# A written-out instruction order, planned anew: head of a hash-attention and feed-forward kernel

## Chip, cores and metric

The kernel runs on one core of one Trainium2 chip. The metric is the device time of one execution in microseconds (us). The kernel before takes 305.61 us (median of 7 runs, 303.85 to 307.07).

## What is computed

For 4 batches, 8 heads, 768 positions and a head width of 64, attention is masked by a hash: query and key may meet only where the signs of their six projections agree. The result is laid out as 4 x 768 rows of 512, and goes through a layer norm, a feed-forward of width 2048 with ReLU, and a residual sum.

```python
q_bits = einsum('bhsd,dk->bhsk', q, proj) > 0        # k_bits likewise
mask   = all six bits of the query equal those of the key
attn   = softmax(where(mask, q @ k.T / 8, -1e9)) @ v
x      = attn as (batch, 768, 512)
out    = x + relu(layernorm(x) * g @ w1) @ w2
```

## The kernel before, in words

**Units and steps.** The output rows are cut into 12 units of 256 rows, three per batch. A unit's attention is six steps: two groups (g) of four heads, and in each three key blocks (kp) of 256 keys. Step s belongs to unit s // 6, group (s % 6) // 3 and key block s % 3; steps 0 to 5 are unit 0, steps 6 to 11 unit 1.

**One step.** `S` (line 443) is 24 matmuls on TensorE: for two halves of the key block, one product of the sign vectors (6 rows, tile G) and two of the values (32 rows each, tiles kb and qb), for four heads. The four heads lie in partitions 0, 32, 64 and 96, so that four matmuls stand in different rows of the array. The sign product raises allowed scores above the others, and the mask thus needs no instruction of its own. `E` (line 449) is the exponential on ScalarE (ACT), two instructions of two heads each. `A` (line 458) is 16 matmuls that add E times V into the PSUM tile `acc`.

**Scores in PSUM.** The scores of a step take two pairs of banks, one for two heads. There are two such pairs, scA and scB. The banks of `acc` can serve as a third pair as long as no sums stand in them; `SC_PAIRS` says for which steps they do.

**Preparing batch 0.** Loads `lx` bring q and k of batch 0 in pieces into tiles X; the vector engine (DVE) transposes a piece of 256 positions in two instructions, `tn` (line 246); `ca` (lines 253 to 257) casts it to bf16, on ACT, POOL (GpSimd) or DVE; `ha` (line 315), four float32 matmuls with the spread projection `pfull`, gives the products whose signs `bi` (line 249, DVE) writes into G. There are 12 such pieces: 2 groups, q or k, 3 blocks. `pf` (line 280, DVE) fills `pfull` from the small load `lp`. `sv` and `sw` sum V over the keys, for a tiny term that keeps the normalisation finite. Later batches use whole loads `LX`, transposes `tu`, casts `CA`, one matmul group `hm` (line 408), `bt`, and 16 small copies `mo` (line 420) into G.

**After a unit's attention** come `na`, `nb`, `nc` (lines 469 to 480; normalising, statistics), `ce` (483, 484), a transpose of the normed rows (on TensorE for unit 0: `ft`, line 498, evicted by `fc`; by DMA later: `fl`, line 493), `F` (line 511; eight matmuls give 256 of the 2048 hidden columns, so eight F per unit), `R` (ReLU, on ACT or DVE), `D` (line 527; four matmuls of the second product), `Z` and the stores `O`. `rs` (489, 490, POOL) is the inverse deviation. `gB` (line 327, word `lg`) is the layer-norm gain, first used by `ce`.

**Weights.** POOL issues eight loads `lw1.p.n` and `lw2.p.n` (lines 330, 333), each 512 KB of bf16 made from float32 on the way. F number p needs chunk p // 2 of w1; D quarter n needs chunk n of w2.

**What sets the order.** The schedule is manual. `ORDER` is a list of words; a word is an operation, an engine (v DVE, a ACT, p POOL, s SP, t TensorE) and its numbers. Each engine runs its words in the order of the list; SP runs the loads, copies and stores that it issues in that order too, and one that waits holds all behind it. Waits between engines follow from the data.

The words of before that start the work:

```
mem.v on.p.1 on.p.0 lp.a pf.v lx.s.0.1.1.3 tn.v.0.1.2 ca.p.0.1.2 tn.v.0.1.1 lx.s.0.0.0.1 tn.v.0.0.0 ca.a.0.0.0
ca.a.0.1.1 lx.s.1.0.0.1 warm.t ha.t.0.1.2 bi.v.0.1.2 tn.v.1.0.0 ca.p.1.0.0 ha.t.0.0.0 bi.v.0.0.0 lx.s.0.1.0.1
```

and how a word is run:

```python
with tc.manual_schedule():
    for word in ORDER.split():
        name, eng, *args = word.split(".")
        OPS[name](ENGINES[eng], *map(int, args))
```

`warm` is 46 small matmuls at the start whose result nobody reads.

Of the kernel before, what the change touches and what calls it, by code (L numbers as in the profile page):

```python
# [17 lines left out]
mem.v on.p.1 on.p.0 lp.a pf.v lx.s.0.1.1.3 tn.v.0.1.2 ca.p.0.1.2 tn.v.0.1.1 lx.s.0.0.0.1 tn.v.0.0.0 ca.a.0.0.0  # L18
ca.a.0.1.1 lx.s.1.0.0.1 warm.t ha.t.0.1.2 bi.v.0.1.2 tn.v.1.0.0 ca.p.1.0.0 ha.t.0.0.0 bi.v.0.0.0 lx.s.0.1.0.1
tn.v.0.1.0 ca.a.0.1.0 ha.t.1.0.0 bi.v.1.0.0 pmem.p p32.p S.t.2.2 E.a.2.1 E.a.2.0 lv.s.0.0.4 cv.p.0.0.2 ha.t.0.1.1  # L20
bi.v.0.1.1 ha.t.0.1.0 lx.s.1.1.0.3 tn.v.1.1.2 ca.p.1.1.2 S.t.1.2 E.a.1.1 E.a.1.0 lx.s.1.0.1.3 ha.t.1.1.2 bi.v.0.1.0
S.t.0.2 E.a.0.0 E.a.0.1 lg.s tn.v.1.1.1 ha.t.1.1.1 ca.p.1.1.1 bi.v.1.1.2 S.t.5.2 E.a.5.1 tn.v.1.1.0 ca.p.1.1.0
ha.t.1.1.0 cv.p.0.0.0 A.t.1.2 A.t.0.2 bi.v.1.1.1 lw1.p.0 E.a.5.0 S.t.4.2 E.a.4.1 lw1.p.1 lx.s.0.0.1.3 tn.v.0.0.2
tn.v.0.0.1 ha.t.0.0.1 ca.v.0.0.1 lw2.p.1 E.a.4.0 bi.v.1.1.0 sv.t.0 LX.s.1.0.1 tu.v.1.0.1.3 tu.v.1.0.1.1 tu.v.1.0.1.2
lw1.p.3 tu.v.1.0.1.0 lw2.p.0 CA.p.1.0.1.1 tn.v.1.0.2 A.t.2.2 bi.v.0.0.1 S.t.6.2 E.a.6.0 E.a.6.1 ha.t.1.0.2 sw.v.0
na.v.0.0 nb.v.0.0 S.t.3.2 nc.v.0.0 E.a.3.1 bi.v.1.0.2 ha.t.0.0.2 lv.s.0.4.4 cv.p.0.4.0 cv.p.0.4.2 sv.t.4 LX.s.1.0.0
tu.v.1.0.0.0 tu.v.1.0.0.2 lv.s.1.4.1 S.t.8.2 E.a.3.0 A.t.3.2 E.a.8.0 A.t.5.2 E.a.8.1 A.t.4.2 ca.v.1.0.2 tn.v.1.0.1
ca.v.1.0.1 bi.v.0.0.2 ha.t.1.0.1 S.t.7.2 E.a.7.1 E.a.7.0 LX.s.1.1.1 lw1.p.2 sw.v.4 na.v.0.1 nb.v.0.1 A.t.8.2
nc.v.0.1 A.t.6.2 ce.v.0.0 bi.v.1.0.1 ft.t.0.0 fc.a.0.0 S.t.10.2 E.a.10.0 E.a.10.1 ce.v.0.1 ft.t.0.1 rs.p.0
tu.v.1.0.0.1 A.t.7.2 fc.v.0.1 F.t.0.0 R.a.0.0 CA.v.1.0.0.0 LX.s.1.1.0 S.t.11.2 E.a.11.1 E.a.11.0 lw2.p.2  # L30
tu.v.1.0.0.3 CA.a.1.0.0.1 hm.t.1.0 bt.v.1.0 mo.s.1.0.3.0 mo.s.1.0.0.0 mo.s.1.0.2.3 mo.s.1.0.0.3 mo.s.1.0.1.2
mo.s.1.0.0.1 mo.s.1.0.1.3 mo.s.1.0.3.3 mo.s.1.0.0.2 F.t.0.7 R.v.0.7 lw2.p.3 S.t.9.2 E.a.9.1 CA.p.1.0.1.0 F.t.0.6
F.t.0.3 na.v.1.0 nb.v.1.0 A.t.10.2 ca.v.0.0.2 E.a.9.0 S.t.14.2 E.a.14.1 tu.v.1.1.0.3 A.t.9.2 R.v.0.6 mo.s.1.0.2.2
E.a.14.0 nc.v.1.0 R.v.0.3 lv.s.1.0.0 A.t.11.2 na.v.1.1 F.t.0.4 R.a.0.4 LX.s.2.1.1 F.t.0.1 R.a.0.1 S.t.13.2 E.a.13.0
E.a.13.1 nb.v.1.1 A.t.14.2 nc.v.1.1 ce.v.1.0 ce.v.1.1 fl.s.1.1 fl.s.1.0 F.t.0.5 R.a.0.5 tu.v.1.1.0.0 lv.s.1.4.2
F.t.0.2 R.a.0.2 LX.s.2.0.0 lv.s.1.4.3 lv.s.1.0.3 tu.v.1.1.0.1 mo.s.1.0.1.1 mo.s.1.0.1.0 mo.s.1.0.2.1 tu.v.1.1.1.3
S.t.12.2 E.a.12.1 E.a.12.0 tu.v.1.1.1.0 tu.v.1.1.0.2 CA.a.1.1.0.1 mo.s.1.0.2.0 lv.s.1.0.1 mo.s.1.0.3.1 LX.s.2.0.1
D.t.0.0.0 D.t.0.0.1 D.t.0.0.2 D.t.0.0.3 S.t.16.2 E.a.16.0 E.a.16.1 mo.s.1.0.3.2 tu.v.1.1.1.1 F.t.1.7 R.v.1.7
A.t.13.2 A.t.12.2 na.v.2.0 F.t.1.2 R.a.1.2 S.t.17.2 E.a.17.1 E.a.17.0 tu.v.1.1.1.2 CA.p.1.1.1.1 hm.t.1.1 Z.v.0.0
D.t.0.1.0 bt.v.1.1 mo.s.1.1.3.2 mo.s.1.1.3.0 mo.s.1.1.2.1 mo.s.1.1.1.1 mo.s.1.1.0.1 mo.s.1.1.0.0 mo.s.1.1.1.2  # L40
mo.s.1.1.3.1 F.t.1.0 R.a.1.0 S.t.15.2 E.a.15.0 E.a.15.1 rs.p.1 nb.v.2.0 nc.v.2.0 A.t.16.2 A.t.17.2 mo.s.1.1.0.3
# [24 lines left out]
tu.v.3.0.1.1 mo.s.2.1.1.1 cv.p.2.0.0 S.t.33.2 E.a.33.0 E.a.33.1 A.t.31.2 sa.p.2.0.2 mo.s.2.1.0.3 tu.v.3.0.1.3
F.t.4.5 R.a.4.5 tu.v.3.0.1.0 tu.v.3.0.0.3 CA.a.3.0.0.1 D.t.3.0.2 D.t.3.0.3 Z.v.3.0 F.t.4.3 R.a.4.3 CA.p.3.0.1.0
rs.p.4 tu.v.3.0.0.0 S.t.35.2 E.a.35.1 E.a.35.0 mo.s.2.1.1.2 F.t.4.6 R.v.4.6 D.t.3.1.0 O.s.2.1 CA.a.3.0.0.0
sa.p.2.0.1 sb.p.2.0 lv.s.2.4.2 lv.s.2.4.3 su.p.2.0 lv.s.2.4.1 lv.s.2.4.0 F.t.4.0 R.a.4.0 S.t.37.2 E.a.37.0 E.a.37.1
na.v.5.0 nb.v.5.0 A.t.35.2 A.t.34.2 nc.v.5.0 O.s.2.3 mo.s.2.1.2.0 F.t.4.2 R.a.4.2 tu.v.3.0.1.2 CA.a.3.0.1.1 A.t.33.2  # L70
na.v.5.1 nb.v.5.1 nc.v.5.1 ce.v.5.1 fl.s.5.1 cv.p.3.4.2 ce.v.5.0 fl.s.5.0 S.t.36.2 E.a.36.1 E.a.36.0 F.t.4.1 R.a.4.1
cv.p.2.4.0 D.t.3.1.1 D.t.3.1.2 D.t.3.1.3 Z.v.3.1 O.s.3.2 O.s.3.1 sa.p.2.4.2 mo.s.2.1.2.3 A.t.36.2 F.t.4.7 R.a.4.7
S.t.38.2 E.a.38.1 F.t.4.4 R.v.4.4 D.t.4.0.0 D.t.4.0.1 E.a.38.0 S.t.42.2 F.t.5.4 R.v.5.4 D.t.4.0.2 D.t.4.0.3 Z.v.4.0
sa.p.2.4.1 F.t.5.3 R.v.5.3 mo.s.2.1.3.3 A.t.38.2 on.p.3 E.a.42.0 sa.p.2.4.0 E.a.42.1 S.t.39.2 E.a.39.1 E.a.39.0
sp.t.2.0 sc.v.2.0 D.t.4.1.0 O.s.3.3 A.t.37.2 na.v.6.0 nb.v.6.0 nc.v.6.0 F.t.5.6 R.a.5.6 S.t.41.2 E.a.41.0 E.a.41.1
D.t.4.1.1 D.t.4.1.2 D.t.4.1.3 Z.v.4.1 O.s.4.1 O.s.4.0 O.s.4.2 O.s.3.0 F.t.5.2 R.a.5.2 S.t.40.2 E.a.40.0 F.t.5.0
R.v.5.0 cv.p.2.4.2 A.t.41.2 lv.s.3.0.1 A.t.39.2 lv.s.3.0.2 F.t.5.1 sb.p.2.4 su.p.2.4 E.a.40.1 S.t.44.2 E.a.44.1
# [42 lines left out]
def kernel(  # L120
# [15 lines left out]
    nc = tc.nc  # L136
    P = 128
    B, H, S, D = q.shape
# [11 lines left out]
    A = 4 * (D + 1)  # L150
    W = S // 4

    SC_PAIRS = {2: ("scA", "scB"), 0: ("acc", "scA"), 1: ("scB", "acc"), 4: ("scA", "scB"), 3: ("acc", "scA"), 5: ("scB", "acc")}
# [15 lines left out]
    p32 = pool.tile([P, 2, 32], F32, name="p32")  # L169
# [421 lines left out]
```

The softmax here doesn't subtract the row's maximum and nothing guards it: scores larger than these inputs give would overflow.

## Time and profile before

| | |
|---|---|
| median of 7 runs | 305.61 us |
| the profiled execution, its own time | 304.04 us |
| its span, first to last instruction | 302.3 us |
| TensorE matmul busy | 292.3 us, 97% |
| ScalarE busy | 194.5 us, 64% |
| VectorE busy | 170.0 us, 56% |
| GpSimd busy | 72.3 us, 24% |
| granted TensorE clock, mean | 1.000 |

PE is TensorE's matmul side, PEld its weight loads, DVE VectorE, ACT ScalarE, POOL GpSimd, SP the engine that issues most DMAs. A row of the timeline gives start and length in us, engine, line, operation, output and inputs, the count, and in brackets the idle time before it and who ended it. Matmuls overlap, so a row's length exceeds the distance to the next row, and a PE that is "busy" is not always at its peak; distances from start to start are the safer measure. "q" after an engine's name is its queue: SPq rows are issues of DMAs.

### The profile page before, as it was taken

The numbers are of one execution on the slowest core, as the hardware profiler recorded it, in microseconds if no ns is written. First come the engines' busy times: TensorE is split into PE (matmuls) and PEld (weight loads), VectorE is DVE, ScalarE is ACT, GpSimd is POOL, SyncE is SP. The second block draws the span as 40 slices with busy tenths as digits, with TensorE's granted clock in tenths as the row PEclk, the third lists the DMA queues.
The fourth block names the chain that finished last, engine by engine and source line by source line (L and its number), as shares of the span: only waits on it lengthen the run. The fifth ranks groups of instructions, "written<-read, shape, count | busy, mean of one in ns | idle before, by whom it ended". The sixth has DMA issues, their size and how long they took to land.

```text
span 302.3 us, 9838 instructions
## 1 busy us (share of the span) xinstructions
PE 292.3 (97%) x4319; PEld 205.0 (68%) x4360; DVE 170.0 (56%) x348; ACT 194.5 (64%) x215; POOL 72.3 (24%) x112
## 2 busy tenths in 40 slices
PE   8999899999999999999999999999999999999994
PEld 7667676675766677676667677776657667685673
DVE  4678878377258527766345767555217446266012
ACT  2977789657667787786567676557667767561320
POOL 2791500202661005241600520911000101001000
PEclk9999999999999999999999999999999999999999
DMA  7999996936164275516306100310402103403122
GB/s 196 376 342 308 208 205 158 263 112 170 47 167 109 55 219 156 103 74 146 87 2 176 38 8 8 75 42 19 89 2 72 37 2 19 105 4 74 30 72 69
DMA packets 30426, 33.58 MB, mean 111 GB/s; under 512 B 15536, under 2 KB 27056, under 8 KB 30384
## 3 DMA queue, kind: packets, MB, share of 16 engines
q1 hardware_dynamic: 25792, 28.50, 35.3%
q0 software_dynamic: 4224, 4.19, 8.5%
q8 instruction: 34, 0.56, 0.8%
q10 hardware_dynamic: 368, 0.26, 0.3%
q14 instruction: 8, 0.07, 0.1%
HBM read 27.53 MB, written 6.29 MB: 112 GB/s over the span
## 4 chain that ended last, share of the span: by engine, by line
PE 88%; DMA 4%; DVE 2%; SPq 2%; ACT 1%; issue 1%; DVEq 0%; ACTq 0%
PE f L511 29%; PE sc L443 17%; PE acc L458 11%; DMA X<-in_q_dram 4%; PE hp L408 3%; ACT E L449 1%; SPq L294 1%; PE f_100None L527 1%; PE f_101None L527 1%; PE f L527 1%; PE f_00None L527 1%; PE f_11None L527 1%; PE f_80None L527 1%; PE f_51None L527 1%; PE f_01None L527 1%
## 5 line engine op out<-in xcount | busy, mean ns | idle before, releaser
L449 ACT ACTIVATE E<-sc,bias_sb 128x1024 bf16<-128x1024 f32 x144 | 153.0, 1110 | 49.2 <-PE sc L443 48.1
L511 PE MATMUL f<-xnT,w_sb 128*128 128x256 bf16 x768 | 99.3, 273 | 0.3
L511 PEld LDWEIGHTS <-w_sb 128*128 128x128 bf16 x768 | 70.9, 98 | 22.9 <-issue 7.7
L519 ACT ACTIVATE hb<-f 128x512 bf16<-128x512 f32 x57 | 33.9, 596 | 44.3 <-PE f L511 44.2
L527 PEld LDWEIGHTS <-hb 128*128 128x128 bf16 x400 | 37.7, 98 | 34.4 <-issue 2.7
L521 DVE TENSOR_SCALAR hb<-f 128x512 bf16<-128x512 f32 x39 | 26.9, 689 | 46.1 <-PE f L511 45.8
L443 PE MATMUL sc<-qb,kb 32*128 32x256 bf16 x1152 | 52.2, 267 | 0.0
L458 PEld LDWEIGHTS <-E 128*128 128x128 bf16 x1152 | 40.0, 98 | 6.4 <-issue 3.8
L458 PE MATMUL acc<-vaug,E 128*128 128x65 bf16 x1152 | 43.4, 194 | 0.1
L443 PE MATMUL sc<-G 6*128 6x256 bf16 x576 | 41.7, 273 | 0.8 <-DVE G L249 0.3
L489 POOL TENSOR_SCALAR rs<-mv 128x2 f32<-128x2 f32 x12 | 7.1, 594 | 104.8 <-DVE mv L483 104.5
L443 PEld LDWEIGHTS <-kb 32*128 32x128 bf16 x1152 | 30.2, 93 | 1.6
L443 PEld LDWEIGHTS <-G 6*128 6x128 bf16 x576 | 15.2, 91 | 18.8 <-issue 15.6
L246 DVE STREAM_TRANSPOSE T<-X 128x384 f32<-128x384 f32 x48 | 24.8, 553 | 3.3 <-DMA X<-in_k_dram 1.1
L469 DVE SCALAR_TENSOR_TENSOR acc<-vsB,acc 128x520 f32<-128x520 f32 x24 | 16.8, 701 | 15.1 <-PE acc L458 14.8
L356 POOL TENSOR_TENSOR t<-vn 128x256 f32<-128x256 f32 x18 | 13.3, 749 | 34.8 <-DMA vn<-in_v_dram 34.6
L346 POOL CAST vaug<-vn 128x768 bf16<-128x768 f32 x16 | 13.1, 829 | 26.5 <-DMA vn<-in_v_dram 21.5
L484 DVE SCALAR_TENSOR_TENSOR xc<-x,mv,gB 128x512 bf16<-128x512 f32 x24 | 18.9, 788 | 0.9
L480 DVE BATCH_NORM_STATS2 st<-x 128x6 f32<-128x256 f32 x48 | 18.0, 417 | 0.7
L476 DVE TENSOR_TENSOR x<-acc,rc 128x512 f32<-128x512 f32 x24 | 16.6, 691 | 0.8
L257 POOL CAST kb<-T 128x768 bf16<-128x768 f32 x10 | 8.4, 841 | 28.6 <-DVE T L246 28.6
L315 PE MATMUL hf<-tp,pfull 128*128 128x256 f32 x48 | 13.2, 401 | 0.4 <-DVE tp L246 0.4
(98 smaller groups left out, 224.1 us busy)
## 6 DMA issues: line engine op xcount, KB each, us to landing
out_dram<-x SPq DMA_DIRECT2D x44, 128.0 KB
X<-in_k_dram SPq DMA_DIRECT2D x7, 768.0 KB
X<-in_q_dram SPq DMA_DIRECT2D x6, 768.0 KB
vn<-in_v_dram SPq DMA_DIRECT2D x24, 192.0 KB
w_sb<-in_moe_w_ch_dram POOLq DMA_DIRECT2D x8, 512.0 KB, 16.6
vn<-in_v_dram SPq DMA_DIRECT2D x2, 768.0 KB
G<-B SPq DMA_DIRECT2D x96, 4.5 KB
X<-in_q_dram SPq DMA_DIRECT2D x2, 512.0 KB
```

Source lines behind the costliest of these rows:

```text
L246: nc.vector.transpose(d[:, j], s[:, j, kj0 : kj0 + n])
L443: nc.tensor.matmul(sc(s, i // 2)[:, i % 2, 256 * kk : 256 * kk + 256], lh, rh, start=(rep == 0), stop=(rep == 2), skip_group_check=True,)
L449: nc.scalar.activation(E(s)[:, heads(h)], sc(s, h), AF.Exp, scale=EXP_SCALE, bias=bias_sb)
L458: nc.tensor.matmul(acc[:, qt, (D + 1) * i : (D + 1) * (i + 1)], E(s)[:, i, 256 * kk + P * qt : 256 * kk + P * qt + P], vaug(u // 3)[:, 4 * ...
L469: nc.vector.scalar_tensor_tensor(acc, vs, EPS_ROW, acc, op0=AOP.mult, op1=AOP.add)
L476: nc.vector.tensor_tensor(xo, a[:, :, :, 0:D], rc.to_broadcast([P, 2, 4, D]), op=AOP.mult)
L480: nc.vector.bn_stats(stats(u)[:, qt, g], xt(u)[:, qt, 256 * g : 256 * g + 256])
L484: nc.vector.scalar_tensor_tensor(xc(u)[:, t], xt(u)[:, t], mv(u)[:, t, 0:1], gB, op0=AOP.subtract, op1=AOP.mult,)
L511: nc.tensor.matmul(f1[:, n].rearrange("p (t x) -> p t x", t=2), w1_sb[:, dt, P * nt : P * nt + P], xnT(u)[:, :, dt], start=(dt == 0), stop ...
L519: nc.scalar.activation(hb(u)[:, 2 * p : 2 * p + 2], f1, AF.Relu)
L521: eng.tensor_scalar_max(hb(u)[:, 2 * p : 2 * p + 2], f1, 0.0)
L527: nc.tensor.matmul(f2, hb(u)[:, nt, P * t : P * t + P], w2_sb[:, nt, half(h)], start=(nt == 0), stop=(nt == NNT - 1),)
```

## The change

The list `ORDER` is replaced as a whole, and `SC_PAIRS` has three entries in place of six. No operation is changed, though some casts, ReLUs and evictions stand on another engine; the new file has one line more, so every line number after the list is one higher. What the new list holds:

- The same units, steps, F, D and stores. Steps 3 and 4 are the only ones whose `S` and `A` are written in head halves: `S.t.3.0 ... S.t.3.1` in place of `S.t.3.2`. A half `S` is 12 matmuls on two of the four row groups.
- The banks of `acc` serve as a third score pair for steps 0, 1 and 2 only. Before, they served for the first six steps, which came in the order 2, 1, 0, 5, 4, 6, 3, 8, 7; now the order is 0, 1, 2, 3, 4, 5, 8, 6, 7.
- SP's first load is now `gB`, which was its eighth. Then come the first q and k blocks of group 0. `pf` now stands behind the first `tn` on DVE. V of group 0 is loaded after all keys of group 1, not before.
- Weights: the issues on POOL come in the order w1.3, w2.1, w1.0, w2.2, w2.3, w1.2, and after `rs` of unit 0 w1.1 and w2.0. Before: w1.0, w1.1, w2.1, w1.3, w2.0, w1.2, and after `rs` w2.2 and w2.3.
- The load of batch 1, group 1, q (`LX.s.1.1.0`) is moved from before the first `mo` copies to behind six of them.
- The first F is `F.t.0.1`, with nine S, seven A and eleven `ha` ahead of it on TensorE; before, `F.t.0.0` had ten S, nine A and twelve `ha` ahead of it.
- The rest of the list, to the last store, is in a new order too; its end has the same form.

```diff
-mem.v on.p.1 on.p.0 lp.a pf.v lx.s.0.1.1.3 tn.v.0.1.2 ca.p.0.1.2 tn.v.0.1.1 lx.s.0.0.0.1 tn.v.0.0.0 ca.a.0.0.0
-ca.a.0.1.1 lx.s.1.0.0.1 warm.t ha.t.0.1.2 bi.v.0.1.2 tn.v.1.0.0 ca.p.1.0.0 ha.t.0.0.0 bi.v.0.0.0 lx.s.0.1.0.1
...
+mem.v pmem.p lg.s lp.a warm.t lx.s.0.0.0.1 tn.v.0.0.0 ca.a.0.0.0 pf.v ha.t.0.0.0 lx.s.0.1.0.1 tn.v.0.1.0 ha.t.0.1.0
+ca.a.0.1.0 p32.p bi.v.0.0.0 bi.v.0.1.0 S.t.0.2 E.a.0.0 E.a.0.1 lx.s.0.1.1.3 tn.v.0.1.1 ha.t.0.1.1 ca.p.0.1.1
+tn.v.0.1.2 ha.t.0.1.2 ca.p.0.1.2 bi.v.0.1.1 S.t.1.2 E.a.1.0 E.a.1.1 lx.s.1.0.0.1 tn.v.1.0.0 ca.p.1.0.0 on.p.0
+bi.v.0.1.2 ha.t.1.0.0 lx.s.1.1.0.3 tn.v.1.1.0 ha.t.1.1.0 ca.p.1.1.0 tn.v.1.1.1 ca.p.1.1.1 tn.v.1.1.2 ca.a.1.1.2
+S.t.2.2 E.a.2.0 E.a.2.1 bi.v.1.1.0 ha.t.1.1.2 bi.v.1.0.0 ha.t.1.1.1 S.t.3.0 E.a.3.0 S.t.3.1 E.a.3.1 lv.s.0.0.4
+cv.p.0.0.2 cv.p.0.0.0 A.t.0.2 A.t.2.2 lw1.p.3 bi.v.1.1.1 S.t.4.0 E.a.4.0 S.t.4.1 E.a.4.1 lw2.p.1 lx.s.0.0.1.3
+tn.v.0.0.1 tn.v.0.0.2 ca.p.0.0.1 ha.t.0.0.1 bi.v.1.1.2 sv.t.0 sw.a.0 lw1.p.0 S.t.5.2 E.a.5.0 E.a.5.1 LX.s.1.0.1
...
+bi.v.0.0.1 sv.t.4 S.t.8.2 E.a.8.1 E.a.8.0 na.v.0.0 nb.v.0.0 A.t.4.0 A.t.3.0 A.t.4.1 nc.v.0.0 A.t.3.1 tu.v.1.0.0.3
+CA.p.1.0.1.1 lv.s.1.4.0 A.t.5.2 LX.s.1.1.1 S.t.6.2 E.a.6.0 E.a.6.1 bi.v.0.0.2 ha.t.1.0.1 CA.p.1.0.1.0 sw.v.4
+na.v.0.1 nb.v.0.1 A.t.8.2 nc.v.0.1 ce.v.0.1 ft.t.0.1 fc.a.0.1 bi.v.1.0.1 ce.v.0.0 rs.p.0 S.t.7.2 E.a.7.0 E.a.7.1
+ft.t.0.0 fc.v.0.0 F.t.0.1 R.v.0.1 F.t.0.6 R.v.0.6 S.t.10.2 E.a.10.1 E.a.10.0 A.t.6.2 CA.a.1.0.0.0 F.t.0.0 R.v.0.0
+A.t.7.2 F.t.0.7 R.v.0.7 S.t.9.2 E.a.9.0 E.a.9.1 tn.v.1.0.2 ca.v.1.0.2 hm.t.1.0 bt.v.1.0 mo.s.1.0.1.0 mo.s.1.0.0.2
...
-    SC_PAIRS = {2: ("scA", "scB"), 0: ("acc", "scA"), 1: ("scB", "acc"), 4: ("scA", "scB"), 3: ("acc", "scA"), 5: ("scB", "acc")}
+    SC_PAIRS = {0: ("scA", "scB"), 1: ("acc", "scA"), 2: ("scB", "acc")}
```

## The prediction

> **What bounds the kernel now.** I read the page's busy shares first, then the chain of waits, then the timeline of the first 36 us, because the chain tells where the changed part stops mattering.
>
> ```profile
> PE 292.3 (97%) x4319; PEld 205.0 (68%) x4360; DVE 170.0 (56%) x348; ACT 194.5 (64%) x215; POOL 72.3 (24%) x112
> ...
> PE 88%; DMA 4%; DVE 2%; SPq 2%; ACT 1%; issue 1%; DVEq 0%; ACTq 0%
> ```
>
> TensorE (PE) is the bound. From 35.6 us on the chain is one matmul group after another:
>
> ```profile
> 55.08 1.05 PE f L511 x8
> 56.13 0.97 PE acc L458 x32
> 57.10 0.87 PE f L511 x8
> 57.97 0.77 PE sc L443 x24
> 58.75 1.44 PE hp L408 x32
> ```
>
> The second column is what each group holds PE for: F 0.87 us, two A 0.97, S 0.77, hm 1.44. Starts follow without a gap, and this lasts to the end of the matmuls. So beyond 36 us an order that keeps PE fed costs the same whatever it is: the same groups at the same prices. What the change can win or lose is settled before the first F: **when it starts, and how much PE work then remains.** The start, from the timeline:
>
> ```profile
> 0.79 0.72 SPq L294 DMA_DIRECT2D X<-in_k_dram  x1
> ...
> 1.11 4.62 PE L289 MATMUL warm<-ones 128*128 128x128 bf16 x46 [1.11 <-DVE ones L261]
> ...
> 2.48 0.70 DVE L280 COPY pfull<-prj 32x12 f32<-32x12 f32 x4 [1.14 <-DMA prj<-in_proj_dram]
> ...
> 5.12 2.08 DVE L246 STREAM_TRANSPOSE tp<-X 128x256 f32<-128x256 f32 x6 [1.94 <-DMA X<-in_k_dram]
> ...
> 5.62 1.13 PE L315 MATMUL hf<-tp,pfull 128*128 128x256 f32 x4
> 5.62 0.92 SPq L327 DMA_DIRECT2D gB<-in_moe_g_ln_dram  x1
> ...
> 9.03 0.29 PE L443 MATMUL sc<-G 6*128 6x256 bf16 x4
> 9.15 0.39 PE L443 MATMUL sc<-qb,kb 32*128 32x256 bf16 x8
> 9.37 0.28 PE L443 MATMUL sc<-G 6*128 6x256 bf16 x4
> 9.48 0.39 PE L443 MATMUL sc<-qb,kb 32*128 32x256 bf16 x8
> ```
>
> The first load (512 KB of keys) lets DVE begin at 5.12; `pfull` is long ready (2.48 + 0.70 = 3.18), and the first `ha` follows the filler matmuls at once, at 5.62. The first S starts at 9.03 with three `ha` done. The first F:
>
> ```profile
> 35.62 1.03 PE L511 MATMUL f<-xnT,w_sb 128*128 128x256 bf16 x8
> ```
>
> How full is PE until then? By 35.62 it has done 12 ha (9.80 to 11.73 holds two: 0.97 each, with hand-over about 1.0), 10 S (7.7 us), 9 A (4.4), 2 sv (1.5) and 2 ft (0.8): 26.4 us of the 30.0 since 5.62. Only 3.6 us are waits. That is all that a better head could win.
>
> **The change, step by step.** I walk the new order along the engines with these rows: tn (two transposes) 0.77 us, bi 0.41, ha to its bi 1.15 (9.80 to 10.97), bi to the next S 0.2 to 0.3, S to its E 0.9 (11.73 to 12.62), an E 1.06 (12.62, 6.28 for six), a POOL key cast 1.09 and query cast 1.52, a V cast 0.83, na 0.70, nb 0.95, nc 0.75, ce 1.0.
>
> 1. *First data.* SP issues gB (256 KB), then the first query block (256 KB): the bytes of before's first load, whose data were there at 5.12. The gB issue takes 0.92 against 0.72, so 5.3. Bounds: 256 KB more or less at the 300 to 390 GB/s of that time are 0.7 to 0.9 us, so 4.5 to 6.1. I take the middle, the nearest row. gB is needed only by ce near 32 us; nothing is gained by having it first.
> 2. *pf behind tn.* DVE does tn to 6.05, then pf 0.70 to 6.75; the first ha starts at 6.9, against 5.62. Only the new place of pf puts its 0.70 on the path.
> 3. *First S.* Two ha to 9.0; the second's bi runs 9.1 to 9.5; S.0 at 9.7. PE waits 0.7 here, and has two ha done, not three.
> 4. *To the halves.* Two ha each go ahead of S.1 (12.5), S.2 (15.4) and S.3.0 (18.2). PE sets the pace; E of step 2 waits for a key cast that is now on ACT (15.6 to 16.7), and ends at 18.8.
> 5. *Halves.* In the rows at 9.03 to 9.48 four heads start together and the next four about 0.11 us later: six foursomes make an S. No row shows two heads alone. Bounds for a half S: 0.34 us, half an S without hand-over, if only the count matters, and 0.67, a whole one, if the 256 columns set the time. I take 0.67, since the 0.11 us between foursomes hardly leaves room for another limit: two steps, +1.34 us, at nothing if two heads go twice as fast. S.4.1 ends at 22.1. The four half A are 32 matmuls as before.
> 6. *To unit 0's end.* ha, sv, S.5 at 23.9, A.1, ha, sv, S.8 at 27.1. E.8 runs 28.0 to 30.1. A.4, A.3 and A.5 end at 29.4; S.6 needs both score pairs and waits for E.8.0: 30.25 (PE idle 0.85). ha, A.8 to 32.55.
> 7. *Norm.* After A.5 DVE does na, nb, nc, ce to 33.0. ft.0.1 at 33.15, S.7 33.6, the other ce to 34.4, ft.0.0, its eviction 35.15 to 35.6; **F.0.1 at 35.75**.
>
> The first F thus comes 0.13 us later than before, and one ha (1.0), one S (0.77) and two A (0.98) fewer lie behind it: 2.75 us are still to be done. 0.13 + 2.75 = **2.9 us more**. A check by waits: 30.1 us lie between 5.62 and 35.75, and the work in them is 11 ha (11.0), 9 S (6.9) and 1.34 for the halves, 7 A (3.4), sv and ft (2.3), 25.0 in all. That leaves 5.1 us of waits against 3.6.
>
> *Weights.* POOL reaches the first weight issue only at 18.9 (two V casts behind two key casts), two us later than before, and the last two stand behind rs of unit 0, as before, at about 35.7.
>
> ```profile
> L333 POOL DMA_DIRECT2D w_sb<-in_moe_w_ch_dram x4: 760/828/867, 18.7 to 35.9; - x4
> ...
> DMA to landing us min/median/max: 11.3/15.2/20.9
> ```
>
> The DMA engines are saturated until 46 us, so bytes ahead count more than the issue: LX.s.1.1.0, 768 KB, now comes after the weights, V loads of 192 KB more come before. w1.0, third, issued about 22, lands near 35; I cost it at nothing, hidden by attention. w1.1 is the thin one: issued at 35.7, with the shortest landing of 11.3 it is there at 47.0, and F.0.2 comes at 45.9 (ten us of S, A, hm, ha and F behind F.0.1). In its queue fewer bytes stand ahead than before; I take no wait, bounds 0 and 1.1 us.
> *SP.* The copies mo start at about 44 behind hm and take 0.77 each; S.20 needs them at 67, and they are out by 63. The transposes fl of unit 1 issue at 53.5 to 56.1, F.1.5 comes at 58.8; before, an issue end to its F was about 2.5 us. Nothing, with 0.3 at most.
>
> [...] The profile's clock row stands at 9 in every slice of before, whose longest PE wait after the filler is 0.6 us; the new order has 1.3 and 0.7 within four. [...]
>
> Against the profiled execution: span 302.3 + 2.9 = 305.2, its time 304.04 + 2.9 = 306.9. The median of the runs shown is 1.57 above that execution, so I forecast 305.61 + 2.9 = **308.5 us**.
>
> **Rivals.**
> - *Hidden cost (no change).* Halves at 0.34 and the query block not held up by gB: 2.9 - 1.34 - 0.8 = +0.8, 306.4 us. For it: PE waits anyway at step 6. Against: S.3 and S.4 start while PE, not ACT, sets the pace. 0.22.
> - *The head at PE's pace (faster).* If no engine holds PE after 5.62, F.0.1 comes at 5.62 + 25.0 = 30.6: 30.6 - 35.62 + 2.75 = -2.3, 303.3 us. It decides for faster where F.0.1 starts before 32.9. Against: the first query block and pf alone take 1.3, E.8 another 0.85. 0.08.
> - *Late w1.1 (slower yet).* F.0.2 waits; with the shortest landing 1.1, so +4.0, 309.6 us; with the median of 15.2 it would wait 5.0, so +7.9, 313.5. 0.15.
> - *The change doesn't do what it says.* "First feed-forward favoured" shows as an earlier F only in the count of groups ahead of it, not in time; this is my forecast itself. 0.55.
>
> **Range and chances.** The forecast's neighbourhood is 0.8 either way for the first data and 1.1 upward for w1.1: 307.7 to 310.4. To leave out no more than 2 in 10 the range must also take in the hidden cost (306.4, less the 0.8 and some scatter of the runs) and, above, a short late wait with late first data: 305.2 to 311.2. Half a per cent, 1.5 us, is about what a measurement here can tell from no change. Faster by more has the head at PE's pace, 0.08; the hidden cost is within it, 0.22; the forecast and late w1.1 are slower, 0.70.
>
> **What would show it.** First ha near 6.9, first S near 9.7, S.3 and S.4 some 1.4 us each, a PE gap before S.6, F.0.1 near 35.75, no gap beyond it. F.0.1 before 33, or halves of 0.35, would prove me wrong; so would gaps on PE after 36 us, which I exclude.

## The result and the profile after

The changed kernel takes **310.67 us** (median of 12 runs, 309.17 to 312.59) against 305.74 us of the kernel before beside it: ratio 1.0166, interval 1.0142 to 1.0189. It is 4.9 us slower by the medians, 5.1 by the ratio; the forecast was 2.9, in a range that ended at 311.2. The profiled execution takes 311.51 us with a span of 309.8, against 304.04 and 302.3: 7.5 us more. This is more than the medians differ by, since before's profiled execution lies 1.7 us below its median and after's 0.8 above. Below, "after" is the changed kernel, and a loss without further words is one in the profiled execution.

The page of after, busy shares and the shares of the chain of waits by engine:

```profile
PE 295.8 (95%) x4317; PEld 207.6 (67%) x4360; DVE 171.6 (55%) x351; ACT 190.0 (61%) x208; POOL 76.9 (25%) x116
...
PE 84%; DMA 7%; DVE 5%; ACT 2%; issue 1%; SPq 1%; ACTq 0%
```

TensorE is still the bound, but of the chain DMA now holds 7% and DVE 5%, where they held 4% and 2%. The list of what PE waited for in the whole of after (in total, times, longest) names the places:

```profile
PE f L512 <- DMA xnT<-xc: 2.3, 1, 2.3
PE warm L290 <- DVE ones L262: 1.1, 1, 1.1
PE hf L316 <- DVE pfull L281: 1.1, 1, 1.1
PE ft L499 <- DVE xc L485: 0.7, 1, 0.7
```

The longest wait is a single one, and it isn't in the first part at all: an F of unit 2 waits 2.3 us for its DMA transposes. I come to it after the start. The timeline of after at the start:

```profile
0.79 0.42 SPq L328 DMA_DIRECT2D gB<-in_moe_g_ln_dram  x1
...
5.90 0.77 DVE L247 STREAM_TRANSPOSE tp<-X 128x256 f32<-128x256 f32 x2 [4.56 <-DMA X<-in_q_dram]
6.59 0.66 DVE L281 COPY pfull<-prj 32x12 f32<-32x12 f32 x4
7.30 3.54 PE L316 MATMUL hf<-tp,pfull 128*128 128x256 f32 x8 [1.10 <-DVE pfull L281]
...
11.36 0.29 PE L444 MATMUL sc<-G 6*128 6x256 bf16 x4 [0.52 <-DVE G L250]
```

The first data come at 5.90 (5.12 before), `pf` follows the first `tn`, and PE waits 1.10 us for it: the first two steps of the forecast, as written, 0.6 and 0.4 us late. But two `ha` then take 3.54 us where two took 1.99 elsewhere. The granted clock goes with it: its record begins with full clock at 10.47 us (at 5.10 before), and until there the matmuls of an `ha` stand 0.43 us apart, against 0.21 in before, which is half clock. S.0 starts at 11.36, 1.7 us behind the forecast. On the way to the first F this lag shrinks to 0.7: **F.0.1 starts at 36.48**, against a forecast of 35.75 and 35.62 before.

Behind the first F, the windows of after from 78 us on (stretch, its length, busy time and instructions of PE, PEld, DVE, ACT, POOL, then the clock, DMA share and GB/s):

```profile
78.00:80.00 2.00, 1.23 (x29) 0.69 (x26) 0.00 (x0) 1.33 (x2) 1.84 (x4) 1.00 1.18 71
80.00:82.00 2.00, 0.46 (x5) 0.42 (x6) 0.00 (x0) 1.38 (x2) 1.92 (x3) 1.00 0.33 71
82.00:84.00 2.00, 2.00 (x10) 0.99 (x8) 0.69 (x1) 0.00 (x0) 1.77 (x5) 0.54 0.31 70
84.00:86.00 2.00, 1.78 (x7) 0.82 (x7) 0.00 (x0) 0.00 (x0) 0.00 (x0) 0.61 0.50 122
```

PE is idle from about 79.2 to 81.54, and then the clock falls to half, by its record from 82.15 to 85.56. The rows of PE around it (one of the eight D matmuls is missing from the trace):

```profile
78.84 0.39 PE L444 MATMUL sc<-qb,kb 32*128 32x256 bf16 x8
81.54 1.34 PE L512 MATMUL f<-xnT,w_sb 128*128 128x256 bf16 x8 [2.31 <-DMA xnT<-xc]
82.67 1.91 PE L528 MATMUL f_10None<-w_sb,hb 128*128 128x512 bf16 x4
84.81 1.19 PE L528 MATMUL f_10None<-w_sb,hb 128*128 128x512 bf16 x3 [0.22 <-issue]
85.83 1.04 PE L512 MATMUL f<-xnT,w_sb 128*128 128x256 bf16 x8
```

From F.2.4 to the next F pass 85.83 - 81.54 = 4.29 us; at full clock, before, an F takes 0.88 (from 77.25) and eight D 1.72 (from 147.65). So half clock costs 1.7 us, half of its 3.41. The 7.5 us are then: 36.48 - 35.62 = 0.86 at the first F; 2.75 of work that now lies behind it, by the prices of the forecast; 2.3 of waiting at F.2.4; 1.7 of half clock. The sum is 7.6. Measured from F.0.1 to the last matmul it is the same: 269.44 us after, 262.88 before, 6.56 more, of which 2.75 is work and **3.8 is lost behind F.0.1**.

What this F waits for, in the timeline of after:

```profile
75.36 2.53 SPq L494 DMA_TRANSPOSE xnT<-xc  x2
```

The two `fl` of unit 2 issue at 75.36 and 76.69. By their landing events in the trace they land 4.85 and 4.81 us after these issues began, at 80.2 and 81.5. The two of unit 1 needed 2.5 and 2.4. Slow ones are not new: in before 10 of the 22 transposes took 3.2 to 4.6 us, without a wait on PE. The questions for the experiments are why these two are slow and what that costs.

### The profile page after: what moved, and what is told of

It is laid out like the page before. It is cut to its first block, busy times and chain, and to the rows that moved or that the text cites. A ratio compares the mean times of both kernels' runs of the same rounds, so it can differ in the third digit from the quotient of the medians.

```text
span 309.8 us, 9840 instructions
## 1 busy us (share of the span) xinstructions
PE 295.8 (95%) x4317; PEld 207.6 (67%) x4360; DVE 171.6 (55%) x351; ACT 190.0 (61%) x208; POOL 76.9 (25%) x116
## 4 chain that ended last, share of the span: by engine, by line
PE 84%; DMA 7%; DVE 5%; ACT 2%; issue 1%; SPq 1%; ACTq 0%
PE f L512 26%; PE sc L444 16%; PE acc L459 10%; PE hf L316 4%; DMA X<-in_q_dram 3%; PE hp L409 2%; DMA vn<-in_v_dram 2%; DMA xnT<-xc 2%; ACT E L450 1%; PE f L528 1%; PE f_71None L528 1%; PE f_90None L528 1%; PE f_81None L528 1%; PE f_21None L528 1%; PE f_101None L528 1%
## 5 line engine op out<-in xcount | busy, mean ns | idle before, releaser
L522 DVE TENSOR_SCALAR hb<-f 128x512 bf16<-128x512 f32 x44 | 30.4, 691 | 60.0 <-PE f L512 59.7
L528 PEld LDWEIGHTS <-hb 128*128 128x128 bf16 x400 | 37.6, 99 | 34.0 <-issue 4.3
L520 ACT ACTIVATE hb<-f 128x512 bf16<-128x512 f32 x52 | 31.0, 596 | 46.2 <-PE f L512 45.9
L444 PE MATMUL sc<-qb,kb 32*128 32x256 bf16 x1152 | 53.0, 267 | 0.0
L444 PEld LDWEIGHTS <-G 6*128 6x128 bf16 x576 | 15.4, 91 | 19.0 <-issue 16.1
L258 POOL CAST kb<-T 128x768 bf16<-128x768 f32 x12 | 9.8, 831 | 41.7 <-DVE T L247 41.7
L485 DVE SCALAR_TENSOR_TENSOR xc<-x,mv,gB 128x512 bf16<-128x512 f32 x24 | 18.0, 752 | 0.9
L316 PE MATMUL hf<-tp,pfull 128*128 128x256 f32 x48 | 14.0, 434 | 1.1 <-DVE pfull L281 1.1
```

The lines of the kernel that those rows point to most:

```text
L316: nc.tensor.matmul(hf(g, t, kp)[:, :256], pfull[:, j], tp(g, t, kp)[:, j], start=(j == 0), stop=(j == 1))
L444: nc.tensor.matmul(sc(s, i // 2)[:, i % 2, 256 * kk : 256 * kk + 256], lh, rh, start=(rep == 0), stop=(rep == 2), skip_group_check=True,)
L485: nc.vector.scalar_tensor_tensor(xc(u)[:, t], xt(u)[:, t], mv(u)[:, t, 0:1], gB, op0=AOP.subtract, op1=AOP.mult,)
L520: nc.scalar.activation(hb(u)[:, 2 * p : 2 * p + 2], f1, AF.Relu)
L522: eng.tensor_scalar_max(hb(u)[:, 2 * p : 2 * p + 2], f1, 0.0)
L528: nc.tensor.matmul(f2, hb(u)[:, nt, P * t : P * t + P], w2_sb[:, nt, half(h)], start=(nt == 0), stop=(nt == NNT - 1),)
```

## The experiments

Each ratio is to the kernel before, timed beside it on the same chip. Words of `ORDER` are shown in the diffs with "..." for what stands between; the changes to after are the whole difference, except for e4. "Lost behind F.0.1" is worked out as above: first F to last matmul, less 262.88 and less 2.75. The 262.88 is from one execution of before, and one below its median, so the column compares these kernels with each other better than with before. Of e8 no diff is shown, as it holds those of e5 and e7; e4, which has other work ahead of its first F, is told in its own place.

| kernel | ratio to before, interval | first F | lost behind F.0.1 | half clock, after the start |
|---|---|---|---|---|
| after | 1.0166 (1.0142 to 1.0189) | 36.48 | 3.8 | 82.15 to 85.56 |
| e1 | 1.0181 (1.0138 to 1.0224) | 36.94 | 3.4 | 37.04 to 40.45 |
| e2 | 1.0148 (1.0109 to 1.0188) | 36.94 | 2.1 | none |
| e3 | 1.0175 (1.0132 to 1.0218) | 37.32 | 3.7 | 7.62 to 11.03, 82.71 to 86.12 |
| e5 | 1.0146 (1.0098 to 1.0195) | 36.63 | 2.2 | none |
| e6 | 1.0202 (1.0151 to 1.0253) | 36.42 | 3.8 | none |
| e7 | 1.0108 (1.0072 to 1.0145) | 34.13 | 3.8 | 79.29 to 82.70 |
| e8 | 1.0160 (1.0107 to 1.0212) | 35.52 | 3.6 | 35.39 to 38.81 |
| e9 | 1.0137 (1.0080 to 1.0195) | 36.55 | 2.9 | 36.23 to 39.64 |
| e10 | 1.0059 (1.0033 to 1.0084) | 34.77 | 1.7 | none |
| e11 | 1.0177 (1.0117 to 1.0237) | 36.38 | 3.6 | 36.09 to 39.51 |
| e12 | 1.0095 (1.0058 to 1.0132) | 33.78 | 3.5 | none |

**e1: a load taken from before the transposes.**

```diff
-... LX.s.3.0.0 ... mo.s.1.1.2.3 mo.s.1.1.0.1 ... fl.s.2.0 ... fl.s.2.1 ...
+... mo.s.1.1.2.3 mo.s.1.1.0.1 ... fl.s.2.0 ... fl.s.2.1 LX.s.3.0.0 ...
```

> The changed kernel with one SP word moved: the 768 KB load LX.s.3.0.0 stands behind the two transposes fl of unit 2 and no longer ahead of them. Theory (that load's packets delay the transposes, F.2.4 waits 2.3 us, and the idle time then costs 3.4 us at half clock): the wait at F.2.4 goes from 2.3 us to under 0.8, no half clock near 82 us, 2 to 4 us less in the profile, 1 to 3.5 us less in the medians (about 307 to 309.5). Rival (SP comes to the transposes too late because of the copies mo ahead of them; the load has no part): F.2.4 still waits at least 1.5 us, the time stays within 1 us of 310.7.

F.2.4 still waits 1.7 us, and the time is that of after. The first transpose landed 2.45 us after its issue, the second, 1.3 us later in the same queue, 4.52. That the load stands ahead of them isn't the cause for both: without it the second is nearly as slow as it was. What begins between their landings is in the trace's list of DMA packets: two packets of the kind "instruction" at 79.5 and 80.2 us, called program packets below.

**e2: the old start.**

```diff
-mem.v pmem.p lg.s lp.a warm.t lx.s.0.0.0.1 tn.v.0.0.0 ca.a.0.0.0 pf.v ha.t.0.0.0 ... lx.s.0.0.1.3 ...
+mem.v pmem.p lp.a warm.t lx.s.0.0.0.1 pf.v tn.v.0.0.0 ca.a.0.0.0 ha.t.0.0.0 ... lx.s.0.0.1.3 lg.s ...
```

> The changed kernel with pf ahead of the first tn on DVE and the gB load put back to eighth place on SP. Theory (these two moves cost the idle PE at the start and leave it at half clock until 10.5 us): first ha at 5.6 to 6.2 in place of 7.3, full clock by 8 us, first S near 9.0 in place of 11.4, F.0.1 at 34.5 to 35.3 in place of 36.5, so 1.2 to 2 us less. Rival (the loss lies in the groups that are still to be done and in the later gap, and the waits for E absorb the start): first S earlier by 2 us, F.0.1 earlier by less than 0.5, time within 0.7 us of 310.7.

The start is mended: first `ha` 5.67, S.0 at 8.14, 3.2 us ahead of after. And F.0.1 is at 36.94, no earlier. The timeline of e2 between them:

```profile
21.99 0.77 DVE L245 STREAM_TRANSPOSE tp<-X 128x256 f32<-128x256 f32 x2 [1.74 <-DMA X<-in_q_dram]
...
25.34 1.50 DVE L245 STREAM_TRANSPOSE T<-X 128x384 f32<-128x384 f32 x3 [2.58 <-DMA X<-in_q_dram]
...
27.21 0.86 PE L367 MATMUL vp<-vaug,ones 128*128 128x260 bf16 x6 [3.04 <-DVE G L248]
```

DVE stands still twice for query loads that nothing urgent needs: `tn.v.1.0.1` and the `tu` of batch 1 are written ahead of `bi.v.0.0.1`, and PE's `sv.4` waits 3.04 us for that `bi`. So what is won at the start is given back at 27 us. This points to the order on DVE, and to when the loads land, as what sets the end of the first part; e7 tries it.

Behind F.0.1 e2 has one wait, 2.2 us at F.2.4, and full clock: 267.71 us to the last matmul, and 265.5 without the wait. That is 2.7 more than in before, so here the forecast's 2.75 of remaining work shows almost alone.

**e3: steps 3 and 4 whole.**

```diff
-S.t.3.0 E.a.3.0 S.t.3.1 E.a.3.1 ... S.t.4.0 E.a.4.0 S.t.4.1 E.a.4.1
+S.t.3.2 E.a.3.0 E.a.3.1 ... S.t.4.2 E.a.4.0 E.a.4.1
```

> The changed kernel with S of steps 3 and 4 whole, both E behind it; the halves of A are left. Theory after the trace (the two halves of a step overlap where they meet, and a step in halves costs PE 0.24 us more than a whole one, the rest being waits for E): F.0.1 within 0.5 us of 36.5, time within 0.7 us of 310.7. Prediction's price (a half costs as much as a whole S, 1.34 us for both steps): 1.3 us less, about 309.4. Third way (whole S waits for both score pairs): 0.5 to 1.5 us more.

Ratio 1.0175, not to be told from after; F.0.1 comes later rather than earlier, at 37.32, though the clock was half in the start of that execution too. Whole, S.4 now waits 0.7 us for an E, so nothing is won. The halves' own price is in after's timeline:

```profile
19.46 0.28 PE L444 MATMUL sc<-G 6*128 6x256 bf16 x2
...
20.15 0.38 PE L444 MATMUL sc<-qb,kb 32*128 32x256 bf16 x4
...
20.47 1.16 PE L459 MATMUL acc<-vaug,E 128*128 128x65 bf16 x32
21.55 0.28 PE L444 MATMUL sc<-G 6*128 6x256 bf16 x2
...
22.50 0.28 PE L444 MATMUL sc<-G 6*128 6x256 bf16 x2
...
23.27 1.13 PE L316 MATMUL hf<-tp,pfull 128*128 128x256 f32 x4
```

The two steps differ. Both halves of S.3 take 20.47 - 19.46 = 1.01 us, 0.24 more than a whole S at 0.77: the second half stands in the two other row groups and begins while the first still runs. In S.4 the second half waits for an E, which ends at 22.46, and begins at 22.50; alone it takes 0.77, as long as a whole S. S.4 takes 23.27 - 21.55 = 1.72 in all, 0.95 more than a whole one. Together the two steps cost 1.19 us more, against 1.34 forecast.

**e4: the old first part, the new rest.** Before's list up to its first F with its six score pairs, then the words of after that are still to do, in after's order:

```diff
-... S.t.0.2 E.a.0.0 E.a.0.1 ... (after's words up to the first F)
+... S.t.2.2 E.a.2.1 E.a.2.0 ... (before's words up to the first F)
...
-    SC_PAIRS = {0: ("scA", "scB"), 1: ("acc", "scA"), 2: ("scB", "acc")}
+    SC_PAIRS = {2: ("scA", "scB"), 0: ("acc", "scA"), 1: ("scB", "acc"), 4: ("scA", "scB"), 3: ("acc", "scA"), 5: ("scB", "acc")}
```

> The order of before up to its first F, with its six steps of bank rotation, then all remaining words in the order of the changed kernel. Theory (the loss is head plus the gap at F.2.4): F starts at 35.6 with ten S and nine A done as before, so 3.6 us of the profiled difference go; if the gap at F.2.4 stays, 2 to 4 us over before, if the shift closes it, within 1 us of before. Rival (the later order itself is slower, in many small waits): 4 us or more over before without a gap of over 1 us.

The first F is at 35.41, as early as before's, with before's work done ahead of it, and still the ratio is 1.0194 (1.0144 to 1.0245). So with the old first part this order is no faster. In its place come a wait of 1.2 us for weights, 0.8 for `hb` in a run of four F, and again 2.1 us at F.2.4; first F to last matmul takes 268.06 us, 5.2 more than in before for the same work. The first two of these waits, at 37.6 and 39.5, stand where the two lists are joined, and after doesn't have them. The rest, 3.2 us, is a sign that **the new order behind the first F has losses of its own**.

**e5: the transposes ahead of a load and two copies.**

```diff
-... LX.s.3.0.0 ... mo.s.1.1.2.3 mo.s.1.1.0.1 ... fl.s.2.0 ... fl.s.2.1 ...
+... fl.s.2.0 ... fl.s.2.1 LX.s.3.0.0 mo.s.1.1.2.3 mo.s.1.1.0.1 ...
```

> The kernel after with one load (LX.s.3.0.0) and two copies (mo) put behind the two DMA transposes fl of unit 2 on SP, so that the transposes issue near 74.1 and 75.4 us in place of 75.36 and 76.69. Theory (a transpose lands 2.4 us after its issue begins, but 3.5 to 4.9 us when a DMA packet of PE's instruction stream starts while its packets run; that packet starts at 78.3 in after): landings near 76.5 and 77.8, F.2.4 starts at once behind S.19, near 79.2 in place of 81.5, no half clock at 82 to 86; 3 to 4 us less than after, ratio to before 1.004 to 1.008. Rival (the transposes are slow there because of the copies and loads around them, wherever they stand): landings still 3.5 us or more behind the issue, F.2.4 still waits 0.8 us or more; at most 1.5 us less than after.

The transposes issue at 74.54 and 75.89. The first lands after 2.47 us; the second after 3.93, for the program packets now start at 77.8 and 78.4. F.2.4 waits 0.4 us and the clock stays full. But S.23 now waits 0.94 us for the copies put behind. The time is 1.0146 of before, which the intervals don't part from after's 1.0166: most of the wait is gone, most of the gain is not there.

**e6: longer filler.**

```diff
-NWARM = 46
+NWARM = 57
```

> The kernel after with 57 filler matmuls in place of 46, which fill the 1.1 us between the end of the filler and the first ha at 7.30. Theory (that gap is why the clock stayed at half until 10.47 us): the clock is full before 8 us, two ha take 2.4 us in place of 3.5, S.0 starts near 10.2 in place of 11.36; but the head waits elsewhere for data, so that F.0.1 moves by less than 0.7 us and the time by less than 1 us. Rival (the head is slow only because of its clock): F.0.1 1.1 us earlier, near 35.3, and the time 1.1 us or more below that of after.

The clock is full at 7.12, two `ha` take 2.0 us, S.0 starts at 9.67, 1.7 us ahead of after; F.0.1 at 36.42, where it was. So the half clock at the start costs nothing at F.0.1, and e2's earlier start didn't move it either. One and the same start differs from kernel to kernel, too: e9, with after's first part and after's filler, has its full clock at 5.51 and S.0 at 9.72.

**e7: the start of e2, and DVE's order.**

```diff
-... tn.v.1.0.1 ha.t.0.0.2 ... LX.s.1.0.0 tu.v.1.0.0.2 tu.v.1.0.0.0 tu.v.1.0.0.1 ... bi.v.0.0.1 sv.t.4 ... nc.v.0.0 ... tu.v.1.0.0.3 ... bi.v.0.0.2 ha.t.1.0.1 ... sw.v.4 ...
+... bi.v.0.0.1 tn.v.1.0.1 ha.t.0.0.2 ... LX.s.1.0.0 ... sv.t.4 ... nc.v.0.0 bi.v.0.0.2 ... ha.t.1.0.1 ... sw.v.4 tu.v.1.0.0.2 tu.v.1.0.0.0 tu.v.1.0.0.1 tu.v.1.0.0.3 ...
```

> The kernel after with the start of e2 (pf ahead of the first tn, gB behind the fourth query load) and DVE's order in the middle of the head changed: bi.v.0.0.1 ahead of tn.v.1.0.1, bi.v.0.0.2 ahead of the norm's second part, the four tu.v.1.0.0 behind sw.v.4. Theory (in e2 the head was held by DVE waiting for the query loads of batch 1 in front of bi.v.0.0.1, 3.0 us at sv.4): that wait goes, F.0.1 starts near 34.5, 2 to 2.5 us before that of after and of e2, and the time is 2 to 2.5 us below that of after; F.2.4 still waits 2 us for its transposes. Rival (the head's end is set by the exponentials or by the last loads, whatever DVE's order): F.0.1 at 36 or later, the time within 1 us of after.

The wait at `sv.4` is gone, and the first F is at 34.13, 2.35 us ahead of after. It waits 1.3 us for w1.0; without that it would be near 33.5, an estimate from e10 and e12, where F.0.1 comes 2.24 us behind the first `ft` (31.23 here). The ratio is 1.0108, 1.8 us below after's; the two intervals barely touch. So DVE's order did bound the first part once the start was early, and behind it stands the weight load that the change put third.

**e8: e5 and e7 together.**

> e5 and e7 together. If the two causes are separate, their gains add: 5.5 us less than after, ratio to before 0.996 to 1.002, F.0.1 near 34.5, no wait at F.2.4. Rival (the fetch packet or the loads move with the head, and the transposes meet them again): F.2.4 or a later F waits 1 us or more for xnT, and the gain is that of e7 alone, 2 to 2.5 us.

The gains don't add. By the median not even e7's gain is left, which the rival expected to stay; the interval holds both. F.0.1 is at 35.52, 1.4 us behind e7's, as an A waits 1.3 us for DVE's `x`. Behind it 3.6 us are lost: 1.6 in a half-clock window at 35.39, 0.9 at F.2.4 for the transposes, and 0.9 at S.23 for its copies.

**e9: other work ahead of F.2.4.**

```diff
-... F.t.2.4 R.v.2.4 ... D.t.1.0.2 D.t.1.0.3 Z.v.1.0 F.t.2.1 R.a.2.1 A.t.20.2 ...
+... D.t.1.0.2 D.t.1.0.3 A.t.20.2 F.t.2.4 R.v.2.4 ... Z.v.1.0 F.t.2.1 R.a.2.1 ...
```

> The kernel after with two quarters of a second matrix product (D.1.0.2, D.1.0.3) and one A (A.20), whose operands are ready by 79.1 us, put ahead of F.2.4 on PE; nothing else moves. 1.72 + 0.49 = 2.2 us of work then stand in the 2.31 us that PE waits for the transposes. Theory (this wait, and the half clock behind it, are 3.7 of the 5 us that after loses): F.2.4 starts near 81.5 with a wait of 0.2 at most, no half clock at 82 to 86, 2.5 to 4 us less than after, ratio to before 1.003 to 1.008. Rival (the wait only moves to another place, the clock falls anyhow): at most 1 us less than after, ratio 1.013 or more.

The transposes are slow (4.37 and 4.07 us), and F.2.4 doesn't notice. F.2.1, now next to F.2.4, waits 0.8 us for `hb`, and a half-clock window came at 36.23. Ratio 1.0137; the interval holds after's.

**e10: e7, e9 and w1.0 ahead of w2.1.**

```diff
-... lw2.p.1 ... lw1.p.0 ...
+... lw1.p.0 lw2.p.1 ...
```

> e7 (start and DVE's order) with e9's order on PE, and with the weight block w1.0 that F.0.1 reads issued ahead of w2.1 on POOL, as in e7 F.0.1 waited 1.3 us for it. Theory (the loss of after is these places and nothing else): F.0.1 near 32.9, F.2.4 without a wait, no half clock between 75 and 90; e7's span of 307.5 less 1.3, 2.3 and 1.4 is 302.5, that of before; ratio to before 0.995 to 1.003. Rival (something further back takes it: the next weights, or the transposes of a later unit): a new PE wait of 1 us or more for w_sb or xnT, ratio 1.006 or more.

This one is clear: 1.0059 (1.0033 to 1.0084), 3.3 us below after, the intervals apart. F.0.1 is at 34.77 without a wait for weights, the transposes of unit 2 are slow (5.0 us) and hidden, no half clock anywhere. It misses the expected 0.995 to 1.003: the first F is 1.9 us later than expected, and F.2.1 waits for `hb`. Of the 1.9 us 1.3 come from a later start (first `ha` at 6.00 against e7's 5.14, S.0 at 8.90 against 7.61), and 0.6 are a wait for the eviction behind `ft`, which the weights had covered in e7. The wait of `ft` for `ce` is there in e7 too:

```profile
PE ft L497 <- DVE xc L483: 1.2, 1, 1.2
...
PE f L510 <- DVE hb L520: 0.8, 1, 0.8
```

Its span is 306.0, 3.7 us above before's: -0.85 at F.0.1, +2.75 of work behind it, +1.7 lost there, 3.6 in sum. By the ratio it is 1.8 us slower than before, which is about what the first two terms give, 1.9.

**e11: the program packets moved.** 138 fillers in place of 46, a quarter as wide:

```diff
-NWARM = 46
+NWARM = 138
...
-            nc.tensor.matmul(wp[:, 0, :P], ones, ones, start=True, stop=True)
+            nc.tensor.matmul(wp[:, 0, :32], ones, ones[:, :32], start=True, stop=True)
```

> The kernel after, its order untouched, with 138 fillers of 32 columns in place of 46 of 128: some 184 more instructions on PE ahead of everything, so that the packets of PE's instruction stream, one in about 256 of its instructions, come about 0.7 of their distance sooner, near 72 and 81 us in place of 78.3. Theory (these packets stretch the transposes of unit 2, which issue at 75.4 and 76.7): both land 2.4 to 2.6 us after their issue begins, by 79.2, F.2.4 waits 0.3 us at most, no half clock behind it; apart from the start, 3 to 4 us less than after. Rival (the transposes are slow for another reason): they land 4 us or more after their issue, and F.2.4 waits 1.5 us or more.

Nothing is touched near 75 us, and the packets come at 72.3 and 82.7. The DMA queues of after while its transposes run (packets, MB, share of 16 engines), from 75.3 to 80.4 us:

```profile
q14 instruction: 1, 0.01, 2.2%
q8 instruction: 1, 0.02, 1.4%
```

In e11 no such packet is there from 76.9 to 80.4 us (one of q14 comes at 80.5, while the second transpose ends), and its timeline reads:

```profile
76.94 2.55 SPq L492 DMA_TRANSPOSE xnT<-xc  x2
...
81.50 1.05 PE L510 MATMUL f<-xnT,w_sb 128*128 128x256 bf16 x8
```

The transposes land 2.94 and 2.42 us after their issues, with the same loads and copies around them, and the wait before F.2.4 is gone. The theory is right about the transposes: with the packets gone from beside them they land on time, and q8's, which came at 78.27 in after, moved with the number of PE's instructions. It is wrong about the time: 1.0177, because a half-clock window came at 36.09, S waits three times for copies (1.1 us in all), and 3.6 us are lost behind F.0.1 as before.

**e12: the start, w1.0 and the moved packets.** e7 with the weight order of e10 and the fillers of e11:

> e7 (start and DVE's order) with w1.0 ahead of w2.1 on POOL, as in e10, but with PE's order untouched and the fillers of e11 in place of e9's exchange. Theory: what is left is the head alone. The time is then that of before's profile + (F.0.1 - 35.62) + 2.75 us for the one ha, one S and two A fewer ahead of F.0.1: e10, with F.0.1 at 34.77, comes to +1.9 by this, and its own new waits at 80 to 83 us (0.8 for hb, 0.2 for bits) and the rest of that stretch made up the other 1.8 of its +3.7. Here F.0.1 is expected at 34.0 to 34.8, the transposes of unit 2 within 3 us, no wait over 0.5 us between 75 and 90: +1.1 to +1.9, span 303.4 to 304.2, ratio to before 1.003 to 1.007. Rival (losses behind F.0.1 belong to the new order itself, not to the transposes): the stretch from 70 to 90 us still loses 1.5 us or more against before, ratio 1.008 or more.

The rival is right about the time, though not about the place. The transposes are within 2.7 us, the clock is full from 4.28 us to the end, F.0.1 is at 33.78, and still 3.5 us are lost behind it: S waits three times for the copies `mo` (1.7 us), an F 0.7 us for weights, a D 0.6 us for `x`. These waits lie between 42 and 208 us; 1.2 us of them are in the stretch from 70 to 90.

```profile
PE sc L442 <- DMA G<-B: 1.7, 3, 0.8
```

Ratio 1.0095 (1.0058 to 1.0132): better than after, not better than e10, and slower than before. No version tried beats before.

## Why the prediction was right, and where it wasn't

**The side and the main term were right.** The kernel is slower, in the range. One `ha`, one S and two A fewer stand ahead of the first F, and nothing behind gives their 2.75 us back: e2 shows 2.7 of it, and e10, with the least losses of its own, still ends 3.7 us later than before though its F.0.1 is 0.85 us earlier. That the time lies in the range is partly luck. The upper end made room for a late w1.1 and late first data; what used it were a wait and a half clock that had no term in the sum.

**Steps 1 and 2** (first data, `pf`): 5.90 and 7.30 against 5.3 and 6.9; the mechanism as written. **Step 3** was mis-sized: S.0 at 11.36 against 9.7, since the clock, which I left out of every term, was half until 10.47. **Steps 4 to 7** start from there: S.1 at 14.06 (12.5), S.2 16.76 (15.4), S.6 31.16 (30.25), F.0.1 36.48 (35.75). The lag shrinks from 1.7 to 0.7, and the start doesn't decide F.0.1: in e2 and e6 S.0 is 3.2 and 1.7 us ahead of after's, and F.0.1 is at 36.94 and 36.42. **Step 5**, the halves, fits in its sum, 1.19 us for 1.34, but not in its parts: S.3's halves overlap (0.24 more than a whole S, not 0.67), and S.4's take 0.95 more, as one of them waits for an E, which the price did not include. So F.0.1 came out within 0.73 us for partly wrong reasons, and that is luck. What bounds it when the start is early was not named: DVE waiting for query loads (e2, e7), then w1.0 (e7), which I had costed at nothing, "hidden by attention". In after it lands at 35.63, 0.85 us ahead of its F.

**The step that failed** is the sentence on "gaps on PE after 36 us, which I exclude", with the bound beside SP: "Nothing, with 0.3 at most". It looked at the `fl` of unit 1 and at one row of before (end of the issue to F, 2.5 us); for unit 1 it holds, F.1.5 does not wait. The second `fl` of unit 2 issues at 73.48 in before, 3.8 us ahead of its first F at 77.25; in after at 76.69, 2.5 us before F.2.4 could start. With that slack a transpose of 4.8 us shows, and landings of up to 4.6 us stood in before's own trace. That beyond 36 us "an order that keeps PE fed costs the same whatever it is" was true, but I didn't check that this one does.

**The rivals.** Late w1.1 did not happen: w1.1 lands at 45.81, F.0.2 starts at 46.85. The hidden cost did not come true: half an S alone takes 0.77 us in S.4, not 0.34, and the first data came at 5.90, later than the 5.3 of the forecast. The head at PE's pace is not reached even by e12 (33.78; it needed 32.9).

**What is settled and what stays open.** Settled: in the profile the 7.5 us are 0.86 + 2.75 + 2.3 + 1.7, within 0.1 (the traces); the slow transposes meet program packets (e11); behind F.0.1 the new order waits in places where before doesn't (e4, e12). By the medians after loses 4.9 us, not 7.5. Half-clock windows differ between executions: in 8 of after's 12 the clock past the start is 0.989 to 0.994 in the mean, with spans of 308.1 to 310.9; in the other four, at 0.999 and 1.0, 307.5 to 308.1. Before's median belongs to a span of about 304.0, so at full clock after is 3.5 to 4.1 us longer, little more than the 0.86 + 2.75 of the first F and the work behind it. e10 has a mean clock below 0.9975 in 2 of 12, e12 in none of 7. Open: how much of the median F.2.4's wait is worth alone. Each of the three kernels that changed little else and took it away (e5, e9, e11) got a new wait or a half-clock window elsewhere, and none is told from after by its interval. It was one wait among several chains with little slack, transposes, copies and `hb`, not the one cause.

## What to carry to other kernels

An order that starts a later stage sooner owes the work it has put off; count it first, it is the safest term. Then go through the new order's tight distances one by one, at every unit and not only next to the edit: from each DMA issue to its first reader, against the slowest landing that the old trace shows, not the median. When removing one wait brings up another of its size, the slack is short in the whole stretch. Here only the kernels with DVE's order mended moved the median clearly, and of them e10, with two more waits taken away, the most; e8, which also joins two mends, did not.

## What the runs showed of the hardware

- **DMA transposes landed late where a program packet of q8 started early in them.** Such a packet has 16 KB and lasts 0.88 to 1.67 us; before and after have 34 each, for 8679 and 8677 instructions of PE on record, weight loads counted. The two traces have 44 transposes. The 18 with no packet of q8 between 2 us before and 4 us after the start of their issue landed 2.43 us after it (median; 16 of them within 2.49, the other two at 2.70 and 3.77). The 9 where one started 0.5 to 1.9 us into the issue took 3.4 to 4.8, median 4.0, so 1.0 to 2.4 us more; in 8 of these 9 no packet of q14 is near. The 4 where it started 3.4 to 3.8 us into the issue took 2.5 at most. In between, at 2.3 to 2.9 us, two of 3 took over 3 us. After's first one of unit 2, with the packet at 2.91, is of these: 13 of its 16 landing events are in by 2.82 us, the other three at 4.83 to 4.85. Of the 10 where the packet started ahead of the issue, six took 2.5 at most, three 3.1 to 3.2 and one 4.55.
- **Half clock past the start lasted 3.41 us each time.** All eight windows in the table have this length. In after's record full clock lasts 71.68 us ahead of the window and 225.28 behind it, 21 and 66 times 3.413; in before 296.96, 87 times. PE was idle for 2.31 us in the 3.41 us ahead of after's fall; in the other stretches of this length, counted from the start of full clock, it was idle for 0.90 at most, in before for 0.86. The length of a wait alone doesn't tell: behind a wait of 2.2 us at F.2.4 e3 and e7 had a half-clock window, and e2 had none. What made that difference is not shown.
- **Two half steps in different row groups overlapped where nothing held the second.** 1.01 us for both against 0.77 for the whole step, in after at 19.46 us; at 22.50, alone, one half took 0.77 too.
